# Attention ahead of two expert layers: value sums moved behind an earlier item's remainder on GpSimd, and half of the q loads moved to ScalarE's queue

## The chip, the cores and the metric

The program runs on one core of one Trainium2 chip. The metric is the device time of one execution in microseconds (us); lower is better. Engines are named as in the profile: PE is TensorE (PEld its weight loads), DVE is VectorE, ACT is ScalarE, POOL is GpSimd, SP is SyncE, which here only issues DMAs. Each engine runs its own instructions strictly in order, so an instruction that waits holds everything behind it on that engine.

## The reference, cut

Two attentions over q, k and v of shape (4, 8, 576, 64) are added: one over groups of four positions (averaged, then repeated four times), one over a band of seven neighbours. The sum goes through a layer of three projections with a maximum, and a layer of two projections with a product.

```python
out_up = np.repeat(sm_attn(q_d, k_d, v_d), 4, axis=2)   # q_d, k_d, v_d: means over 4 positions
mask = np.abs(pos[:, None] - pos[None, :]) < 4
scores = np.where(mask, scale * q @ k.T, -1e9)
out_local = softmax(scores) @ v
x = (out_up + out_local).transpose(0, 2, 1, 3).reshape(2304, 512)
h = np.maximum(np.maximum(x @ w1, x @ w2), x @ w3) @ w_out
out = ((h @ w_a) * (h @ w_b)) @ w_out2
```

## The kernel before

The attention is cut into 16 items, one for each batch and pair of heads. An item goes through five steps: `a_load_qk` and `a_load_v` issue its loads, `a_qk` makes transposed q and k and their sums over four, `a_scores` makes both score matrices and the softmax, `a_tr` transposes the probabilities and sums the values over four, `a_av` makes the weighted values, adds both attentions into `x32` and splits the sum into a rounded part `xh` (on ACT) and a remainder `xl` (on POOL). The main loop writes the steps of several items interleaved (`LOOP`, `LOOPS`); a list scheduler with its own timing model then sets the order on each engine. Pieces of the first expert layer's weights are loaded (`raw`), converted on DVE, ACT and POOL (`w_step`), and the first layer's matmuls for finished blocks of x (L700, through `early` and `fill`) stand between the attention's matmuls on PE. After the attention comes the rest of both layers, in an order written out by hand.

Items 8 to 15 load q and k already blocked for a transpose on DVE: four DMAs for k and four for q per item, of 72 KB each, in runs of 32 numbers (L228); items 0 to 7 are transposed on PE and take three DMAs for each (L236, L239). In the kernel before every load of the attention is issued from SP's queue. Buffers are few: the tiles q, k, vr and vw have one buffer in each of two pools, which even and odd items take in turn (`pool2`). Items 9, 11, 13 and 15 use a third pool, `ex2`, that no item before 9 uses. So a load of item i + 2 waits for the last reader of item i, and item 9 waits for nobody.

The values of an item stand in `vr` (for the sums over four) and `vw` (for the band). On POOL two additions sum vr: L419 adds the four rows in pairs, in place, and L420 adds the two halves into `vd`, which PE then reads (L456). The other work on POOL in this part: `ed` (L401) and `el` (L408) normalise the probabilities that PE then transposes (L430, L441), `xl` (L502) is the remainder, L567 the low part of a converted weight.

All loads count their completion on eight counters in turn, whichever queue issues them, and a load waits until the one eight places ahead of it in the program has landed. `tc.issue_after(x)` tells the scheduler to place what stands inside it behind instruction x.

Of the kernel before, what the change touches and what calls it, by code (L numbers as in the profile page):

```python
# [15 lines left out]
ALU = mybir.AluOpType  # L16
# [19 lines left out]

SPLIT_AFTER = {0: 1}
CB = 1

ACT_LOADS = 0  # L40
W2B = 4
# [23 lines left out]
def attn_moe_kernel(  # L65
# [14 lines left out]
    nc = tc.nc  # L80
# [35 lines left out]
    def nq(t):  # L116
        return min(QT, S - t * QT)
# [12 lines left out]
    def bk(st, name):  # L130
        if 1 in psp_:
            return psp_[1].tile([P, 512], F32, tag="m", name=name, bufs=4)
        t, n = ("t", 3) if st in "tv" else ("m", 5)
        return psp_[0].tile([P, 512], F32, tag=t, name=name, bufs=n)
# [25 lines left out]
    for half in range(2):  # L160
        m = cap[half * 64 : half * 64 + 64]
        for sgn in (1, -1):
            nc.gpsimd.affine_select(
                out=m,
# [26 lines left out]
    def xtiles(blk):  # L191
        if blk not in xh:
            pl = xps[blk // HB]
            xh[blk] = pl.tile([P, NK, TB], F32R, tag="xh", name="xh")
            xl[blk] = pl.tile([P, NK, TB], F32R, tag="xl", name="xl")
        return xh[blk], xl[blk]

    def pool(i, n):

        return ex if i < NI // 2 and i % n == n - 1 else ap_  # L200

    def pool2(i):

        return ex2 if i >= NI // 2 and i % 2 else pool(i, 2)

    def pieces(b):
        t0, done = b * S, 0
        while done < S:
            blk, o = divmod(t0 + done, TB)
            n = min(S - done, TB - o)  # L210
            yield done, n, blk, o
            done += n
# [4 lines left out]
    def a_load_qk(i):  # L217
        b, hp = items[i]
        s = st[i]
        h = 2 * hp  # L220
        engs = (nc.sync, nc.scalar if i < ACT_LOADS else nc.sync)
        if i >= TV:
            for nm, src in (("k", k), ("q", q)):
                x = pool2(i).tile([P, (RF + 1) * 2 * D], F32, tag=nm, bufs=1, name=nm)
                s[nm] = x[:, :S]
                for j in range(P // BS):
                    hh, d0 = divmod(j * BS, D)
                    nc.sync.dma_start(  # L228
                        x[j * BS : (j + 1) * BS, :S].rearrange("p (c d) -> p c d", d=BS),
                        src[b, h + hh, :, d0 : d0 + BS].rearrange("(c p) d -> p c d", p=BS),  # L230
                    )
            return
        for eng, nm, src in zip(engs, "kq", (k, q)):
            s[nm] = pool2(i).tile([P, RF + 1, 2, D], F32, tag=nm, bufs=1, name=nm)
            for j in range(2):
                eng.dma_start(  # L236
                    s[nm][:, :RF, j, :], src[b, h + j, : RF * P].rearrange("(r p) d -> p r d", p=P)
                )
            eng.dma_start(  # L239
                s[nm][:RT, RF], src[b, h : h + 2, RF * P :].rearrange("h p d -> p h d")  # L240
            )
# [45 lines left out]
    mark = {}  # L287
# [41 lines left out]
    def half_of(j, t):  # L329

        return 1 - j if t >= NP2 else j
# [83 lines left out]
    def a_tr(i):  # L415
        s = st[i]
        s["vd"] = ap_.tile([DK, NDK, 2, D], F32, tag="vd", bufs=2, name="vd")
        vr = s["vr"].rearrange("p h c f d -> p (h c) f d")
        nc.gpsimd.tensor_tensor(out=vr[:, :, 0:2, :], in0=vr[:, :, 0:2, :], in1=vr[:, :, 2:4, :], op=ALU.add)  # L419
        nc.gpsimd.tensor_tensor(  # L420
            out=s["vd"].rearrange("p c h d -> p h c d"),
            in0=s["vr"][:, :, :, 0, :],
            in1=s["vr"][:, :, :, 1, :],
            op=ALU.add,
        )
        ptd = s["ptd"] = pool2(i).tile([DK, NDK, NDQ * 2 * DQ], F32, tag="ptd", bufs=1, name="ptd")
        for c in range(NDK):
            ps = bk("t", "ps_td")
            for t in range(NDQ):
                nc.tensor.transpose(  # L430
                    ps[:DK, t * 2 * DQ : (t + 1) * 2 * DQ],
                    s["ed"][:, t, c * DK : (c + 1) * DK],
                    ident[: 2 * DQ, : 2 * DQ],
                )
            nc.scalar.copy(ptd[:, c, :], ps[:DK, : NDQ * 2 * DQ])
        pt = s["pt"] = []
        for u0 in range(0, NP2, TG):
            ps = bk("t", "ps_tl")
            n = min(TG, NP2 - u0)
            for u in range(n):  # L440
                nc.tensor.transpose(  # L441
                    ps[:, u * P : (u + 1) * P],
                    s["el"][:, 2 * (u0 + u) : 2 * (u0 + u) + 2, :].rearrange("m a x -> m (a x)"),
                    ident,
                )
            x = pool(i, 2).tile([P, TG, P], F32, tag="pt", bufs=3, name="pt")
            nc.scalar.copy(x[:, :n].rearrange("m t k -> m (t k)"), ps[:, : n * P])
            pt.append(x)

    def a_av(i):  # L450
        b, hp = items[i]
        s = st[i]
        ps = bk("v", "ps_ud")
        for c in range(NDK):
            for j in range(2):
                nc.tensor.matmul(  # L456
                    ps[64 * j : 64 * j + 64, :SD],
                    s["vd"][:, c, j, :],
                    s["ptd"][:, c, :].rearrange("m (t h i) -> m t h i", t=NDQ, h=2)[:, :, j],
                    start=(c == 0),  # L460
                    stop=(c == NDK - 1),
                )
        FH = FAC // 2
        up = pool(i, 2).tile([P, SD * 2, 1], F32, tag="up", bufs=1, name="up")
        nc.scalar.activation(
            out=up[:, :, 0].rearrange("m (g f) -> m g f", f=2),
            in_=ps[:, :SD].unsqueeze(2).to_broadcast([P, SD, 2]),
            func=AF.Copy,
            scale=1.0 / FAC,
        )  # L470
        x32 = pool(i, 2).tile([P, S], F32, tag="x32", bufs=1, name="x32")
        pss = [bk("v", "ps_av") for _ in AVG]
        for u in range(NP2):
            for j, r in ((0, 0), (1, 1), (1, 0), (0, 1)):
                t = r * NP2 + u
                half = half_of(j, t)
                rr = slice(r * KW, (r + 1) * KW)
                nc.tensor.matmul(  # L478
                    pss[r][64 * j : 64 * j + 64, u * QT : u * QT + nq(t)],
                    s["vw"][rr, j, u, :],  # L480
                    s["pt"][u // TG][rr, u % TG, half * 64 : half * 64 + nq(t)],
                    start=True,
                    stop=True,
                )
        for (g0, g1), ps in zip(AVG, pss):
            a0, a1 = g0 * QT, min(g1 * QT, S)
            if i in ADD_PSUM:
                mark['d', i] = nc.vector.tensor_tensor(
                    out=x32[:, a0:a1].rearrange("m (g f) -> m g f", f=FH),
                    in0=ps[:, : a1 - a0].rearrange("m (g f) -> m g f", f=FH),  # L490
                    in1=up[:, a0 // FH : a1 // FH].to_broadcast([P, (a1 - a0) // FH, FH]),
                    op=ALU.add,
                )
            else:
                nc.scalar.copy(x32[:, a0:a1], ps[:, : a1 - a0])
        if i not in ADD_PSUM:
            xg = x32.rearrange("m (g f) -> m g f", f=FH)
            mark['d', i] = nc.vector.tensor_tensor(out=xg, in0=xg, in1=up.to_broadcast([P, SD * 2, FH]), op=ALU.add)
        for o, n, blk, bo in pieces(b):
            a, l = xtiles(blk)  # L500
            nc.scalar.copy(a[:, hp, bo : bo + n], x32[:, o : o + n])  # L501
            nc.gpsimd.tensor_tensor(  # L502
                out=l[:, hp, bo : bo + n],
                in0=x32[:, o : o + n],
                in1=a[:, hp, bo : bo + n].bitcast(F32),
                op=ALU.subtract,
            )
        st[i] = None
# [18 lines left out]
    def convert_steps(key, w=None):  # L527
# [5 lines left out]
        pl = late["p"] if late_n[0] % 2 else rawp  # L533
        e = pl.tile([P, NP_], U16, tag="ce", name="ce", bufs=CB)
        fin = w
        if w is None or "c" not in psp_:
            m = pl.tile([P, NP_], F32, tag="cm", name="cm", bufs=CB)
            if w is None:
# [849 lines left out]
    def emit(f, i):  # L1388
        if i < NI and (f, i) not in emitted:
            emitted.add((f, i))  # L1390
            {"k": a_load_qk, "v": a_load_v, "Q": a_qk, "S": a_scores, "T": a_tr, "A": a_av}[f](i)
# [9 lines left out]
    for i in range(NI):  # L1401
# [4 lines left out]
        for x in LOOPS.get(i, LOOP).split():  # L1406
            f, d = x[0], int(x[1:])
# [121 lines left out]
    for n, (c, p) in enumerate(units):  # L1529
# [105 lines left out]
        if turn or p == 2:  # L1635
            x = 0 if turn else c + 1
# [38 lines left out]
```

## Time and profile before

| what | us |
|---|---|
| median of 3 runs | 848.06 (846.41 to 849.10) |
| the profiled execution, as timed | 848.16 |
| its span, first to last instruction | 846.4 |
| PE busy | 818.0 (97%) |
| DVE / POOL / ACT busy | 650.9 / 441.0 / 355.6 |

The timed value of the profiled execution is 1.8 us over its span and 0.1 us over the median. The attention ends near 200 us; from there on nearly all of the chain that ended last is PE. Where PE stands idle is in the first 110 us.

### The profile page before, as it was taken

The page shows a single profiled execution, that of the slowest core. Times are in us where ns is not written, and L with a number is a line of the kernel's source. Part 1 is how long each engine was busy: PE and PEld are TensorE (multiplying, and loading weights), DVE is VectorE, ACT ScalarE, POOL GpSimd, SP SyncE. Part 2 cuts the span into 40 slices and gives each one's busy share as a digit, 9 for nine tenths or more (in the row PEclk, how much of TensorE's full clock was granted, in tenths as well). Part 3 has the DMA queues.
Part 4 walks back from the last instruction along what each step waited for, and adds up shares of the span by engine and source line. Part 5 has one row for each costly group of instructions (what it writes and reads, how often), then busy time and mean ns, then how long its engine had stood idle before and what let it go on. Part 6 is the DMA issues. An engine that isn't in the chain of part 4 may idle for free.

```text
span 846.4 us, 15417 instructions
## 1 busy us (share of the span) xinstructions
PE 818.0 (97%) x5785; PEld 767.2 (91%) x5785; DVE 650.9 (77%) x1220; ACT 355.6 (42%) x812; POOL 441.0 (52%) x417
## 2 busy tenths in 40 slices
PE   5988799999999999999999999999999999999998
PEld 3767589999999999999989999999999999999997
DVE  4896986754989688689689689798888745577775
ACT  4785555544343223324246543444443432333331
POOL 3876586535456335546557645545554543355541
PEclk9699989999999999999999999999999999999999
DMA  7899975200321111320144554454442358766612
GB/s 175 182 191 163 171 124 110 43 21 2 124 75 50 51 50 50 137 75 26 68 156 174 189 189 168 179 187 171 178 174 106 143 207 330 259 225 224 225 51 74
DMA packets 125555, 116.33 MB, mean 137 GB/s; under 512 B 81834, under 2 KB 108202, under 8 KB 125482
## 3 DMA queue, kind: packets, MB, share of 16 engines
q1 hardware_dynamic: 121162, 98.06, 39.9%
q10 hardware_dynamic: 4320, 17.30, 5.7%
q8 instruction: 45, 0.74, 0.4%
q14 instruction: 28, 0.23, 0.1%
HBM read 80.74 MB, written 34.60 MB: 136 GB/s over the span
## 4 chain that ended last, share of the span: by engine, by line
PE 86%; DMA 5%; DVE 3%; POOL 3%; issue 1%; SPq 1%; ACT 1%; POOLq 0%; DVEq 0%; ACTq 0%
PE ps_m L700 40%; PE ps_u L1091 30%; PE ps_q L865 5%; PE ps_m L1241 4%; DMA vr<-in_v_dram 2%; PE ps_av L478 1%; PE ps_tl L441 1%; DMA raw<-in_moe_w_out_dram 1%; PE ps_ud L456 1%; PE ps_s L358 1%; PE ps_sd L340 1%; PE ps_m L865 1%; DMA vw<-in_v_dram 1%; POOL vr L419 1%; PE ps_td L430 1%
## 5 line engine op out<-in xcount | busy, mean ns | idle before, releaser
L700 PE MATMUL ps_m<-xh,w 128*128 128x384 f32 x864 | 173.7, 339 | 0.3 <-ACT xh L501 0.3
L700 PEld LDWEIGHTS ps_m<-xh,w 128*128 128x128 f32 x864 | 151.2, 189 | 1.7 <-ACT xh L501 0.6
L1091 PE MATMUL ps_u<-xh,w 128*128 128x384 f32 x720 | 136.8, 336 | 0.1
L1091 PEld LDWEIGHTS ps_u<-xh,w 128*128 128x128 f32 x720 | 125.3, 188 | 1.9 <-DVE acc L756 0.5
L1091 PE MATMUL ps_u<-xl,w 128*128 128x384 f32 x648 | 122.5, 335 | 0.4 <-ACT sn L1103 0.4
L1091 PEld LDWEIGHTS ps_u<-xl,w 128*128 128x128 f32 x648 | 112.9, 188 | 2.2 <-ACT sn L1103 0.7
L1103 ACT COPY sn<-ps_u 128x384 f32<-128x384 f32 x108 | 51.2, 479 | 123.5 <-PE ps_u L1091 120.3
L1281 POOL TENSOR_TENSOR gl<-g,gh 128x384 fp32r<-128x384 f32 x52 | 54.7, 1053 | 83.3 <-ACT gh L1280 83.3
L700 PE MATMUL ps_m<-xl,w 128*128 128x384 f32 x432 | 94.4, 337 | 0.2 <-POOL xl L502 0.2
L700 PE MATMUL ps_m<-wo,gh 128*128 128x512 f32 (+1 forms) x316 | 92.4, 390 | 0.0
L700 PEld LDWEIGHTS ps_m<-xl,w 128*128 128x128 f32 x432 | 76.5, 188 | 0.9 <-POOL xl L502 0.4
L700 PEld LDWEIGHTS ps_m<-wo,gh 128*128 128x128 f32 x316 | 58.4, 188 | 9.6
L729 DVE TENSOR_TENSOR t<-ps_m,t 128x384 f32<-128x384 f32 x48 | 26.4, 551 | 45.1 <-PE ps_m L700 38.4
L1022 POOL TENSOR_TENSOR w<-F,w 128x768 fp32r<-128x768 f32 (+1 forms) x36 | 56.3, 1578 | 9.2 <-ACT w L1020 8.7
L551 ACT ACTIVATE ce<-ce,ebias 128x512 int16<-128x512 uint16 x60 | 43.4, 723 | 41.0 <-DVE ce L544 41.0
L1350 DVE TENSOR_TENSOR acc<-ps_m,acc 128x512 f32<-128x512 f32 (+1 forms) x67 | 45.0, 677 | 18.7 <-PE ps_m L700 18.4
L554 DVE SCALAR_TENSOR_TENSOR ce<-raw,ce 128x512 uint16<-128x512 uint16 x60 | 49.8, 830 | 3.6 <-ACT ce L551 3.5
L1115 DVE TENSOR_TENSOR ca<-ps_u,sn 128x384 f32<-128x384 f32 x54 | 30.0, 555 | 28.8 <-PE ps_u L1091 17.9
L1033 POOL TENSOR_TENSOR F<-F 128x256 f32<-128x256 f32 x24 | 20.1, 839 | 59.3 <-DVE F L561 49.5
L700 PE MATMUL ps_m<-wo,gl 128*128 128x512 f32 (+1 forms) x158 | 48.9, 391 | 0.0
L1233 DVE TENSOR_TENSOR acc<-ps_m,acc 128x512 f32<-128x512 f32 (+1 forms) x62 | 33.3, 552 | 15.4 <-PE ps_m L1241 13.1
L544 DVE TENSOR_SCALAR ce<-raw 128x512 uint16<-128x512 uint16 x60 | 39.1, 652 | 2.1 <-DMA raw<-in_moe_w_dram 1.7
(209 smaller groups left out, 1684.6 us busy)
## 6 DMA issues: line engine op xcount, KB each, us to landing
dw<-w SPq DMA_DIRECT2D x24, 768.0 KB
raw<-in_moe_w_dram SPq DMA_DIRECT2D x18, 512.0 KB
raw<-in_moe_w_out_dram SPq DMA_DIRECT2D x18, 512.0 KB
w<-dw SPq DMA_DIRECT2D x12, 768.0 KB
w<-dw ACTq DMA_DIRECT2D x12, 768.0 KB
dw<-wo SPq DMA_DIRECT2D x12, 512.0 KB
vw<-in_v_dram SPq DMA_DIRECT2D x62, 80.0 KB
vr<-in_v_dram SPq DMA_DIRECT2D x16, 288.0 KB
```

Of the source, the lines that this page charges most:

```text
L544: nc.vector.tensor_scalar(out=e, in0=top, scalar1=0x7FF0, scalar2=None, op0=ALU.bitwise_and)
L551: nc.scalar.activation(out=s16, in_=e, func=AF.Relu, bias=ebias, scale=8.0)
L554: nc.vector.scalar_tensor_tensor(out=e, in0=top, scalar=0x8000, in1=e, op0=ALU.bitwise_and, op1=ALU.bitwise_or)
L700: nc.tensor.matmul(ps, lhs[a], rhs[b], start=(i == 0), stop=(i == n - 1))
L865: nc.tensor.matmul(ps, sw[c0, n][a][:, m * P : (m + 1) * P], hq[n][b], start=start and k == 0, stop=k == 2, skip_group_check=not start,)
L1022: nc.gpsimd.tensor_tensor(out=l, in0=w, in1=h.bitcast(F32), op=ALU.subtract)
L1091: nc.tensor.matmul(ps, w[:, a, slot, kk], y[:, b * HK + kk], start=start and i == 0, stop=i == 3 * HK - 1, skip_group_check=not start,)
L1103: nc.scalar.copy(t, ps)
L1233: nc.vector.tensor_tensor(out=a, in0=x, in1=a, op=ALU.add)
L1241: nc.tensor.matmul(y, lhs[a], tw[c, n][b], start=start and k == 0 and t == ts.start, stop=k == 2, skip_group_check=True,)
L1281: nc.gpsimd.tensor_tensor(out=l, in0=g, in1=h.bitcast(F32), op=ALU.subtract)
L1350: nc.vector.tensor_tensor(out=a, in0=ps, in1=a, op=ALU.add)
```

## The change

First, from item 6 on (`VR_AFTER`) both value additions of item i are placed behind the last remainder `xl` of item i - 2. Second, the four q loads of each of the items 8 to 15 are issued from ACT's queue; the k loads stay on SP's. No instruction is added or removed but the queue of 32 DMAs is another, and the scheduler orders all engines anew up to the end of the attention.

```diff
+VR_AFTER = 6
@@ a_load_qk, items 8 to 15
-                    nc.sync.dma_start(
+                    (nc.scalar if nm == "q" else nc.sync).dma_start(
@@ a_tr
-        nc.gpsimd.tensor_tensor(out=vr[:, :, 0:2, :], in0=vr[:, :, 0:2, :], in1=vr[:, :, 2:4, :], op=ALU.add)
-        nc.gpsimd.tensor_tensor(
...
+        after = ExitStack()
+        if i >= VR_AFTER:
+            after.enter_context(tc.issue_after(mark["x", i - 2].ins))
+        with after:
+            nc.gpsimd.tensor_tensor(out=vr[:, :, 0:2, :], in0=vr[:, :, 0:2, :], in1=vr[:, :, 2:4, :], op=ALU.add)
+            nc.gpsimd.tensor_tensor(
...
@@ a_av
-            nc.gpsimd.tensor_tensor(
+            mark["x", i] = nc.gpsimd.tensor_tensor(
                 out=l[:, hp, bo : bo + n],
```

POOL, from the normalisation of item 6 on (vr_1105 is item 6, vr_1304 item 7, vr_1638 item 9; x32_905, x32_1074 and x32_1220 are the sums of items 3, 4 and 5; line numbers of the changed kernel are six higher here). Before:

```order
L401 TENSOR_TENSOR ed_1015<-ed_1015,sd_1018 96x432
L419 TENSOR_TENSOR vr_1105<-vr_1105 72x4x128
L408 TENSOR_TENSOR el_1016<-el_1016,sl_1020 128x5x64 x2
L502 TENSOR_TENSOR xl_429<-x32_905,xh_428 128x384
L502 TENSOR_TENSOR xl_433<-x32_905,xh_432 128x192
L419 TENSOR_TENSOR vr_1304<-vr_1304 72x4x128
L419 TENSOR_TENSOR vr_1638<-vr_1638 72x4x128
L420 TENSOR_TENSOR vd_1415<-vr_1105 72x2x2x64
L567 TENSOR_TENSOR w6_781<-cm_1125,w6_780 128x512
L401 TENSOR_TENSOR ed_1277<-ed_1277,sd_1280 96x432
L502 TENSOR_TENSOR xl_433<-x32_1074,xh_432 128x192
L502 TENSOR_TENSOR xl_1102<-x32_1074,xh_1101 128x384
```

Now:

```order
L410 TENSOR_TENSOR el_1016<-el_1016,sl_1020 128x5x64 x2
L508 TENSOR_TENSOR xl_429<-x32_905,xh_428 128x384
L508 TENSOR_TENSOR xl_433<-x32_905,xh_432 128x192
L403 TENSOR_TENSOR ed_1277<-ed_1277,sd_1280 96x432
L410 TENSOR_TENSOR el_1278<-el_1278,sl_1282 128x5x64 x2
L403 TENSOR_TENSOR ed_1388<-ed_1388,sd_1391 96x432
L573 TENSOR_TENSOR w6_781<-cm_1125,w6_780 128x512
L508 TENSOR_TENSOR xl_433<-x32_1074,xh_432 128x192
L508 TENSOR_TENSOR xl_1102<-x32_1074,xh_1101 128x384
L425 TENSOR_TENSOR vr_1105<-vr_1105 72x4x128
L410 TENSOR_TENSOR el_1389<-el_1389,sl_1393 128x5x64 x2
L426 TENSOR_TENSOR vd_1415<-vr_1105 72x2x2x64
```

The additions of item 6 moved from ahead of item 3's remainder to behind item 4's; those of items 7 and 9 stood ahead of a weight piece, an `ed` and item 4's remainder and are no longer there.

SP at the very start, with the counters that each load waits for. Before:

```order
L236 DMA q<-in_q_dram 128x4x64 x2
L239 DMA q<-in_q_dram 64x2x64
L236 DMA k<-in_k_dram 128x4x64 x2
L239 DMA k<-in_k_dram 64x2x64 [waits DMAHW0_49]
L236 DMA q<-in_q_dram 128x4x64 [waits DMAHW1_49]
```

Now:

```order
L238 DMA q<-in_q_dram 128x4x64
L238 DMA q<-in_q_dram 128x4x64 [waits DMAHW0_49]
L241 DMA q<-in_q_dram 64x2x64 [waits DMAHW1_49]
L238 DMA k<-in_k_dram 128x4x64 [waits DMAHW2_49]
L238 DMA k<-in_k_dram 128x4x64 [waits DMAHW3_49]
L241 DMA k<-in_k_dram 64x2x64 [waits DMAHW4_49]
```

Item 9's four q loads now stand first on ACT's queue and take the counters 0, 3, 5 and 7, so the second q load of item 0 waits for the first of them.

ACT between the exponentials of item 6 and those of item 7. Before:

```order
L376 ACTIVATE ed,eps_119<-ps_sd,md 96x144 x3
L465 ACTIVATE up<-ps_ud 128x288
L566 CAST w_780<-cm 128x512
L395 ACTIVATE el<-el 128x5x64
L435 COPY ptd<-ps_td 72x288
L395 ACTIVATE el<-el 128x5x64
L283 ACTIVATE qd_95<-qp 64x3x48 x2
```

Now:

```order
L378 ACTIVATE ed,eps_119<-ps_sd,md 96x144 x3
L397 ACTIVATE el<-el 128x5x64
L230 DMA q<-in_q_dram 32x18x32
L441 COPY ptd<-ps_td 72x288
L397 ACTIVATE el<-el 128x5x64
L230 DMA q<-in_q_dram 32x18x32
L507 CAST xh<-x_905 128x384
L507 CAST xh<-x_905 128x192
L230 DMA q<-in_q_dram 32x18x32
L441 COPY ptd<-ps_td 72x288
L557 ACTIVATE ce<-ce,ebias 128x512
```

The q loads of item 10 now stand between the copies and exponentials; the first of them waits for DVE to have read item 8's q, and each for the load eight places ahead of it.

## Rows read from the trace of the kernel before

**Rows 1.** The page's part 2: busy tenths in 40 slices of 21.2 us.

```profile
PE   5988799999999999999999999999999999999998
PEclk9699989999999999999999999999999999999999
```

**Rows 2.** Stretches of 10 us: busy time of each engine, granted clock, DMA share, GB/s.

```profile
0.00:10.00 10.00, 3.29 (x13) 2.43 (x14) 1.85 (x4) 3.31 (x7) 6.00 (x24) 1.00 0.55 127
...
60.00:70.00 10.00, 10.00 (x156) 8.03 (x159) 8.55 (x24) 7.83 (x25) 6.13 (x8) 1.00 1.04 164
70.00:80.00 10.00, 8.85 (x122) 7.08 (x114) 5.96 (x14) 6.37 (x20) 5.66 (x8) 1.00 0.91 160
80.00:90.00 10.00, 5.18 (x95) 3.95 (x95) 8.82 (x19) 1.90 (x5) 6.24 (x7) 0.95 0.94 161
90.00:100.00 10.00, 9.67 (x130) 7.83 (x127) 9.06 (x21) 6.38 (x20) 7.00 (x7) 0.88 0.93 166
100.00:110.00 10.00, 7.43 (x36) 6.07 (x36) 10.00 (x23) 5.79 (x19) 7.24 (x8) 0.80 1.13 190
110.00:120.00 10.00, 10.00 (x127) 8.37 (x126) 7.80 (x22) 6.84 (x22) 8.25 (x10) 0.86 0.56 117
```

**Rows 3.** Waits, POOL alone, 60 to 110 us: total, times, longest.

```profile
POOL vr L419 <- DMA vr<-in_v_dram: 12.2, 4, 4.0
```

**Rows 4.** Timeline of POOL: start, us, instruction [idle before, releaser].

```profile
68.16 1.28 POOL L419 TENSOR_TENSOR vr<-vr 72x512 f32<-72x512 f32 x1 [3.87 <-DMA vr<-in_v_dram]
...
76.04 1.27 POOL L419 TENSOR_TENSOR vr<-vr 72x512 f32<-72x512 f32 x1 [3.72 <-DMA vr<-in_v_dram]
77.93 1.28 POOL L419 TENSOR_TENSOR vr<-vr 72x512 f32<-72x512 f32 x1 [0.62 <-DMA vr<-in_v_dram]
...
79.87 1.27 POOL L567 TENSOR_TENSOR w<-cm,w 128x512 fp32r<-128x512 f32 x1
81.10 0.91 POOL L401 TENSOR_TENSOR ed<-ed,sd 96x432 f32<-96x432 f32 x1
...
102.76 1.86 POOL L419 TENSOR_TENSOR vr<-vr 72x512 f32<-72x512 f32 x1 [3.97 <-DMA vr<-in_v_dram]
104.58 1.40 POOL L408 TENSOR_TENSOR el<-el,sl 128x320 f32<-128x320 f32 x2
```

**Rows 5.** Timeline of DVE.

```profile
81.18 1.11 DVE L547 TENSOR_SCALAR cm<-raw 128x512 uint32<-128x512 uint32 x1 [3.56 <-POOL w L567]
```

**Rows 6.** Timeline of PE: where it stood idle.

```profile
4.38 1.09 PE L309 MATMUL ps_t<-ident,k 128*128 128x128 f32 x4 [4.38 <-DMA k<-in_k_dram]
6.13 1.09 PE L309 MATMUL ps_t<-ident,q 128*128 128x128 f32 x4 [0.67 <-DMA q<-in_q_dram]
...
82.06 0.44 PE L430 MATMUL ps_td<-ident,ed 96*72 96x96 f32 x3 [0.95 <-POOL ed L401]
...
88.81 0.30 PE L345 MATMUL ps_s<-cap,identb 128*128 128x320 bf16 x1 [3.50 <-DVE el L392]
...
106.04 1.33 PE L441 MATMUL ps_tl<-ident,el 128*128 128x128 f32 x5 [2.45 <-POOL el L408]
```

**Rows 7.** Timeline of SP's queue: start, us of issuing.

```profile
0.74 0.99 SPq L236 DMA_DIRECT2D k<-in_k_dram  x2
...
2.53 1.14 SPq L236 DMA_DIRECT2D q<-in_q_dram  x2
...
60.28 1.20 SPq L228 DMA_DIRECT2D q<-in_q_dram  x2
61.57 2.07 SPq L228 DMA_DIRECT2D k<-in_k_dram  x4
63.74 0.42 SPq L248 DMA_DIRECT2D vr<-in_v_dram  x1
64.26 3.07 SPq L272 DMA_DIRECT2D vw<-in_v_dram  x4
67.37 3.31 SPq L228 DMA_DIRECT2D q<-in_q_dram  x6
70.78 1.67 SPq L248 DMA_DIRECT2D vr<-in_v_dram  x2
...
85.84 2.35 SPq L228 DMA_DIRECT2D q<-in_q_dram  x4
```

More of the change, by code (lines that the diff above doesn't have):

```diff
@@ L418, in a_tr @@
         vr = s["vr"].rearrange("p h c f d -> p (h c) f d")
-        nc.gpsimd.tensor_tensor(out=vr[:, :, 0:2, :], in0=vr[:, :, 0:2, :], in1=vr[:, :, 2:4, :], op=ALU.add)
-        nc.gpsimd.tensor_tensor(
[L421 to L425, printed above, removed]
+        after = ExitStack()
[4 more added lines that the diff above has]
+            nc.gpsimd.tensor_tensor(
+                out=s["vd"].rearrange("p c h d -> p h c d"),
+                in0=s["vr"][:, :, :, 0, :],
+                in1=s["vr"][:, :, :, 1, :],
+                op=ALU.add,
+            )
         ptd = s["ptd"] = pool2(i).tile([DK, NDK, NDQ * 2 * DQ], F32, tag="ptd", bufs=1, name="ptd")
```

## The prediction

> **What bounds the kernel now.** I read the page's slices first, then ten-microsecond stretches, then who waited for whom on POOL, DVE and PE, and last the timelines of POOL and SP around PE's idle places. The slices [rows 1] show PE full nearly everywhere but in the first five, some 106 us; that is the attention's first half. After 110 us PE has no room (10.00 of 10 us busy in the last stretch of [rows 2]), so a load or a POOL wait that gets shorter there moves nothing. What can be won lies before. In the stretches from 60 to 110 us PE is busy 10.00 + 8.85 + 5.18 + 9.67 + 7.43 = 41.1 of 50 us, so it is idle 8.9 us, and the granted clock falls to means of 0.95, 0.88, 0.80 and 0.86 from 80 to 120 us: parts of these stretches ran at 1.2 instead of 2.4 GHz, after idle pieces of 3.50 and 2.45 us [rows 2, 6]. If PE could use the whole of it, that would be (0.05 + 0.12 + 0.20 + 0.14) x 10 = 5.1 us more.
>
> Where do the idle pieces come from? Three of them, 0.95, 3.50 and 2.45 us, sum to 6.90 us [rows 6]. The reader should follow each back. At 102.76 POOL starts a value addition after 3.97 us of waiting for its load; `el` stands behind it and starts at 104.58, and PE starts on it at 106.04 [rows 4, 6]. At 76.04 and 77.93 two value additions wait 3.72 and 0.62 us; behind them stand a weight piece (79.87) and an `ed` (81.10). PE waited for that `ed` until 82.06. DVE waited 3.56 us for that weight piece, until 81.18 [rows 4, 5, 6], and everything on DVE behind it came later, the `el` for which PE waited until 88.81 among it. So additions whose loads came late held, on an in-order engine, work that was ready: 12.2 us of waiting in four places [rows 3]. The second thing to see is SP's queue. From 60.28 to 72.45 us its rows follow each other with gaps near 0.1 us: it issues all the time, at some 0.5 us for each load [rows 7]. The loads of vr come late because they stand in that row.
>
> **The change part by part.**
>
> The value additions from item 6 on. The order of POOL shows that items 6, 7 and 9 no longer stand ahead of `el`, the weight piece, `ed` and the remainders of items 3 and 4. Their two instructions still cost the same on POOL; what goes is the wait in front. By that time the vr load, issued long before, should have landed. Value: the three idle pieces of PE, -6.90 us. At the lower end of the gain stands 0, when what PE then waits for is the next late thing (k, vw or q through the same SP queue). The upper end is 6.90 + 5.1 = 12.0 us, if PE also keeps its clock. Queued behind the additions on POOL are now `el` and `hl`, and vd waits for them; PE needs vd of item i only after xl of item i - 2 and a whole item in between, so I cost that at nothing. It has one more reader: the vr load of item i + 2 waits for vd of item i, and on SP everything behind that load waits too. If that cover is gone the price is one such load, from 63.74 to the addition at 68.16, so 4.4 us [rows 4, 7].
>
> The q loads off SP. Each q load costs SP 1.20 / 2 to 3.31 / 6, near 0.57 us [rows 7]; a stretch of 60 to 73 us holds eight, 4.5 us. I give this no gain of its own. It is what lets vr, vw and k land sooner, so that the 6.90 us are really won and not turned into waits for loads.
>
> Here a rule speaks against the change. The row first: the DMA engines are busy for shares of 0.91 to 1.13 in these stretches, at 160 to 190 GB/s [rows 2]. The Trainium skill, DMA: Bandwidth & Descriptors, section Issuing engines are not separate DMA queues, says that loads started from several engines run on the same 16 DMA engines, and that a second issuer saves only the sequencer's time, which is "usually small relative to the DMA itself". By that rule the loads would land no sooner; SP's rows without gaps speak for the opposite, that issuing is the bound here. What the rule would make of the time is the first rival.
>
> The q loads onto ACT. No row shows such a load on ACT in this part. Of the 32, some 17 (four each of items 8, 10, 11, 12 and one more) fall before 110 us. At 0.5 us, SP's price for one, they take 8.5 us of ACT, which is busy 7.83 + 6.37 + 1.90 + 6.38 + 5.79 = 28.3 of 50 us from 60 to 110 us [rows 2] and has 21.7 us to spare. Most fall into gaps; but ACT is in order, and one load of each item stands ahead of a copy (ptd or pt) that PE reads. Five items by 0.5 us give +2.5 us, which I take, because ACT's spare time is well over the 8.5 us; the bounds are 0 and 8.5 us. What is queued behind: the copies and exponentials shown for items 6 and 7, and PE and DVE wait for these.
>
> The start. Item 9's q loads need no buffer to come free, so the scheduler put them first of all, on ACT, and the second q load of item 0 now waits for the first of them through the counters. Before, k of item 0 was issued from 0.74 and PE had it at 4.38; q was issued at 2.53 and, its second load, near 2.53 + 1.14 / 2 = 3.1, and PE had it at 6.13 [rows 6, 7]. If ACT's first load lands like k, near 4.3, the second q load starts 1.2 us later, and all of SP's queue behind it too. Value +1.2 us, since PE and DVE wait for loads all through the start. The bounds are 0 and 3.5 us: 4 x 72 KB more at 127 GB/s [rows 2] take 2.3 us, if nothing of the DMA engines' idle share (0.55 busy) hides them.
>
> **The sum** against the profiled execution's own 848.16 us (0.1 us over the median): 848.16 - 6.90 + 2.5 + 1.2 = 844.96. I forecast **845.0 us**, faster by 3.1 us or 0.37%. A measurement of this kernel can tell about 0.3%, 2.5 us, from no change, so this is close to that line.
>
> **The rivals.**
>
> First: the transfers are the bound, and the gain is used up by waits for loads. For it speak the DMA shares, and that DVE, too, is busy 42.4 of these 50 us [rows 2]; against it SP's rows without gaps. Then the 6.90 us are not won, the start costs 1.2 us, and the stretch from 60 us loses the four q loads of item 9, now at the start: 4 x 72 KB at 160 GB/s, 1.8 us. 848.16 + 1.2 - 1.8 = 847.6: no change. This is also the time by the skill's rule.
>
> Second, on the other side: ACT's in-order queue takes over the part that POOL had. A q load on ACT waits for the landing of the load eight places ahead, most of which SP issues, and for DVE's reading of the q two items back. When ACT gets there before SP's load has landed, it stands still, and with it exponentials and copies. A landing under load took 4.4 us (63.74 to 68.16) [rows 4, 7]. It decides from the point where the three items 10 to 12 lose together more than the 6.90 us, or 2.3 us each, half a landing. Then the wait is only handed on: 848.16 + 2.5 + 1.2 = 851.9, slower. For it: the loads stand amid exponentials, and SP is the late queue now. Against it: ACT has 21.7 us to spare, and SP is relieved.
>
> Third: the new order at the start costs its upper 3.5 us and the gain is halved: 848.16 - 3.45 + 2.5 + 3.5 = 850.7. That the change does not do what it says is excluded by the order of instructions.
>
> **How the numbers follow.** Forecast 0.52 (of that 0.46 below the line and 0.06 within), first rival 0.24 (0.02 faster, 0.18 same, 0.04 slower), second 0.16 and third 0.08 (together 0.03 same, 0.21 slower). Faster 0.48, same 0.27, slower 0.25. The range goes down to 848.16 - 12.0 + 2.5 + 1.2 = 839.9 and up to the second rival, 851.9; the tails beyond (ACT's bound of 8.5 us on top of the start) I hold for under 2 in 10.
>
> **What would show it.** Right: in the changed profile POOL's waits for vr between 60 and 110 us go from 12.2 us to under 3; PE's idle time in that stretch falls below 4 us; the stretches from 110 us look as before, but some 3 to 4 us earlier. PE's first transposes of q start 1 us or so later than 6.13. ACT's own queue shows issues of some 0.5 us, each with little wait ahead. Wrong: POOL's waits vanish and PE's idle time stays, with q, k or vw as the releaser (first rival); ACT stands idle ahead of q loads and PE waits for ptd, pt or qd (second); or the first 60 us take 3 us or more longer (third).

## The result, and the profile after

The changed kernel takes **856.62 us** (856.05 to 857.85) against 847.93 us before: ratio 1.0103, 95% interval 1.0085 to 1.0121, so it is slower by 8.7 us. The forecast was 845.0 us, with a range up to 851.9.

Where the time went is read best in three stretches. First the kernel before, then the changed one; columns as in [rows 2].

```profile
0.00:60.00 60.00, 45.69 (x548) 34.67 (x549) 46.30 (x118) 37.28 (x116) 37.91 (x57) 0.83 0.86 183
60.00:110.00 50.00, 41.13 (x516) 32.97 (x517) 42.39 (x99) 28.27 (x87) 32.27 (x36) 0.93 0.99 168
110.00:160.00 50.00, 50.00 (x605) 45.03 (x607) 37.23 (x96) 26.88 (x72) 31.70 (x37) 0.97 0.51 98
```

```profile
0.00:60.00 60.00, 38.20 (x461) 29.62 (x461) 41.00 (x105) 32.14 (x101) 33.38 (x52) 0.86 0.91 177
60.00:110.00 50.00, 43.90 (x577) 34.40 (x578) 43.47 (x104) 31.28 (x96) 32.26 (x36) 0.88 0.98 158
110.00:160.00 50.00, 46.69 (x537) 41.51 (x536) 35.15 (x82) 24.32 (x66) 28.93 (x34) 0.91 0.67 102
```

PE, the first number behind the comma, loses 7.5 us of busy time in the first 60 us, wins 2.8 us from 60 to 110, where the gain was forecast, and loses 3.3 us from 110 to 160, where before it had no idle time at all. Together that is 8.0 us, nearly the whole difference. The mean granted clock, the third number from the end, is lower than before in the second and third stretch too (0.88 against 0.93, 0.91 against 0.97), and no run shows what that adds. The slices, which answer [rows 1], show the thinner start too:

```profile
PE   4679899999999999999999999999999999999998
PEclk9889779999999999999999999999999999999999
```

What was forecast for POOL came true. Its two largest waits between 60 and 110 us (total, times, longest), and two of its moved additions (they answer [rows 3, 4]):

```profile
POOL el L410 <- DVE sl L409: 6.9, 3, 2.9
POOL xl L508 <- ACT xh L507: 5.1, 4, 2.4
```

```profile
90.75 1.28 POOL L425 TENSOR_TENSOR vr<-vr 72x512 f32<-72x512 f32 x1
...
100.11 1.53 POOL L425 TENSOR_TENSOR vr<-vr 72x512 f32<-72x512 f32 x1
```

In that stretch no addition waits for its load any more; before it was 12.2 us. The start came as described, too. ACT, SP and PE (the latter answers [rows 6]):

```profile
0.73 2.19 ACTq L230 DMA_DIRECT2D q<-in_q_dram  x4
```

```profile
2.54 1.83 SPq L238 DMA_DIRECT2D q<-in_q_dram  x2
```

```profile
4.92 1.09 PE L311 MATMUL ps_t<-ident,k 128*128 128x128 f32 x4 [4.92 <-DMA k<-in_k_dram]
7.52 1.12 PE L311 MATMUL ps_t<-ident,q 128*128 128x128 f32 x4 [1.51 <-DMA q<-in_q_dram]
...
29.83 1.03 PE L311 MATMUL ps_t<-ident,k 128*128 128x128 f32 x4 [3.30 <-DMA k<-in_k_dram]
```

The first two q loads of item 0 take 1.83 us to issue instead of 1.14, for the second waits for the counter, and PE's first transposes of q start 1.39 us later than before. But item 0's remainder on POOL starts at 42.21 us instead of 34.23:

```profile
42.21 1.79 POOL L508 TENSOR_TENSOR xl<-x,xh 128x384 fp32r<-128x384 f32 x2
```

That is 8 us, not 1.4. That gap is what the experiments had to explain.

### The profile page after: what moved, and what is told of

The parts are those of the page before. It is cut to its first block, busy times and chain, and to the rows that moved or that the text cites. A ratio compares the mean times of both kernels' runs of the same rounds, so it can differ in the third digit from the quotient of the medians.

```text
span 855.1 us, 15412 instructions
## 1 busy us (share of the span) xinstructions
PE 819.1 (96%) x5785; PEld 768.8 (90%) x5785; DVE 652.9 (76%) x1220; ACT 354.6 (41%) x812; POOL 441.0 (52%) x417
## 4 chain that ended last, share of the span: by engine, by line
PE 83%; DMA 6%; DVE 5%; issue 2%; POOL 2%; ACT 1%; SPq 1%; ACTq 0%; DVEq 0%; POOLq 0%
PE ps_m L706 39%; PE ps_u L1097 30%; PE ps_q L871 4%; PE ps_m L1247 4%; DMA vr<-in_v_dram 1%; DMA raw<-in_moe_w_dram 1%; DMA k<-in_k_dram 1%; DMA raw<-in_moe_w_out_dram 1%; PE ps_s L360 1%; PE ps_sd L342 1%; PE ps_m L871 1%; PE ps_av L484 1%; DMA q<-in_q_dram 1%; DMA vw<-in_v_dram 1%; PE ps_td L436 1%
## 5 line engine op out<-in xcount | busy, mean ns | idle before, releaser
L550 DVE TENSOR_SCALAR ce<-raw 128x512 uint16<-128x512 uint16 x60 | 41.3, 688 | 5.2 <-DMA raw<-in_moe_w_out_dram 4.0
```

Of the source, the lines that this page charges most:

```text
L550: nc.vector.tensor_scalar(out=e, in0=top, scalar1=0x7FF0, scalar2=None, op0=ALU.bitwise_and)
```

## Experiments

Ratios are to the kernel before, measured beside each run on the same chip; its median there was 846.6 to 847.9 us, so 0.1% is 0.85 us.

| run | q loads on ACT | additions moved | ratio | 95% interval |
|---|---|---|---|---|
| changed kernel | 8 to 15 | yes | 1.0103 | 1.0085 to 1.0121 |
| e1_vr_only | none | yes | 0.9928 | 0.9913 to 0.9943 |
| e2_q_only | 8 to 15 | no | 1.0082 | 1.0064 to 1.0101 |
| e3_q9_on_sp | 8, 10 to 15 | yes | 0.9983 | 0.9974 to 0.9992 |
| e5_only_q9 | 9 | no | 1.0127 | 1.0097 to 1.0156 |
| e7_q9_old_order | 9 | no, old order | 0.9991 | 0.9976 to 1.0006 |
| e8_new_order_no_q9 | none | no, order of e5 | 1.0141 | 1.0121 to 1.0162 |
| e10_one_place | none | no, one place of it | 1.0028 | 1.0013 to 1.0043 |
| e14_first_42 | none | no, first 42 us of it | 1.0039 | 1.0024 to 1.0054 |
| e15_first_100 | none | no, first 100 us of it | 1.0105 | 1.0085 to 1.0124 |
| e4_q9_held | 8 to 15, 9 late | yes | 0.9993 | 0.9979 to 1.0007 |
| e9_vr_q12 | 12 to 15 | yes | 0.9953 | 0.9935 to 0.9971 |
| e11_order_q_on_sp | none | yes, order of e3 | 0.9935 | 0.9916 to 0.9953 |
| e12_adds_alone | none | yes, old order else | 0.9939 | 0.9923 to 0.9956 |
| e13_vr_from_4 | none | from item 4 | 0.9954 | 0.9935 to 0.9973 |
| e16_q_order_adds | 8 to 15 | yes, order of e2 else | 1.0124 | 1.0104 to 1.0143 |

### Which part costs

The changed kernel taken apart: the additions alone, the q loads alone, both but for item 9's q, and item 9's q alone.

```diff
@@ e1_vr_only
-                    (nc.scalar if nm == "q" else nc.sync).dma_start(
+                    nc.sync.dma_start(
@@ e2_q_only
-VR_AFTER = 6
+VR_AFTER = 99
@@ e3_q9_on_sp
+                    (nc.scalar if nm == "q" and i != 9 else nc.sync).dma_start(
@@ e5_only_q9 (and VR_AFTER = 99)
+                    (nc.scalar if nm == "q" and i == 9 else nc.sync).dma_start(
```

> Only the value additions are moved (from item 6 on behind the remainder of the item two back); all q loads stay on SP. Before 847.9 us, changed 856.6 us. Theory A (the loss is made in the first 42 us by item 9's q loads, which start the program on ACT; the additions are worth what the trace of the changed kernel wins back between items 4 and 6, 3 to 5 us): 843 to 846 us. Theory B (the loss comes from q loads standing on ACT's in-order queue after 60 us): also 843 to 846 us, so this run does not part A from B. Theory C (the moved additions lose, since the vr and vw loads behind them on SP come later): 850 to 854 us.

> Only the q loads of items 8 to 15 are moved to ACT; the value additions are placed as before. Theories A and B: 857 to 861 us, all of the loss and without the gain of the additions. Theory C (the additions lose): 848 to 851 us.

> Both parts, but item 9's four q loads stay on SP, so ACT's queue starts without a load; items 8 and 10 to 15 load q from ACT. Theory A: the first 42 us are as before (item 0's remainder starts near 34.2 us on POOL, not 42.2) and the time is 844 to 848 us. Theory B: the start is as before, but ACT still waits with q loads after 60 us and the time is 852 to 857 us.

> The kernel before with one thing changed: item 9's four q loads on ACT, where they come first of all; everything else stays on SP and the additions stay where they were. Theory A: item 0's remainder starts 6 to 8 us later than 34.2 and most of that reaches the end: 853 to 857 us. Theory B: the start costs 1 to 2 us and the time is 848 to 850 us.

Measured: 840.75, 853.34, 844.98 and 857.24 us against 846.66. The additions alone gain 0.7%, 6.1 us by the ratio (5.9 between the medians), more than theories A and B had for them. Item 9's four q loads alone, the smallest edit of all, cost 1.3%: theory A in the time, and item 0's remainder starts at 41.62 us, 7.4 later; with those four on SP again it starts at 34.95. That the loss is made in the first 42 us, as theory A has it, is not shown by this, and comes out otherwise below. The other q loads on ACT cost too, from 0.9928 to 0.9983, so theory B has a share as well. Theory C falls for the additions alone, but comes back below. The q loads alone met no theory: at 853.34 us they cost less than A or B had, and less than item 9's four by themselves. The parts don't simply add; each of these kernels has an order of its own.

### Is it the loads, or the order?

Item 9's loads change two things: what is transferred at the start, and the order that the scheduler makes for everything else. A pair of kernels parts them. Every instruction of the attention is chained, engine by engine, to a given list; the loads at issue are left out of it. (Line numbers in chained kernels are some 240 higher, as the list stands ahead of the code.)

```diff
+        for names in ORDER:
+            last = None
...
+                    if last is not None:
+                        tc.add_manual_dep(i, last.name, dep, reason="order")
+                    last = i
```

> The kernel before with item 9's four q loads first on ACT's queue, as in the run that moved only them, but every other instruction of the attention is chained to the order that it has in the kernel before, engine by engine. Before is 846.7 us and the run with these loads and the scheduler's own order 857.2 us. Theory O (the new order is what costs; the loads themselves delay the start by 1.3 us, which DVE's backlog has swallowed by 17 us): 846 to 850 us. Theory L (the loads cost, by the transfer volume and the shared counters): 853 to 858 us.

> The other half of the same pair: no load stands on ACT, item 9's q loads are at their usual place on SP, but every other instruction of the attention is chained to the order that the scheduler makes when item 9's q loads come first. Theory O (the order costs): 853 to 858 us, with item 0's remainder on POOL 6 to 8 us later than 34.2. Theory L (the loads cost): 845 to 849 us.

The loads with the old order: 0.9991, no cost that can be told. The new order without the loads: 1.0141, 12 us, a little more than expected. Theory O holds on both sides. PE in the kernel with the loads and the old order, and after it the kernel before:

```profile
7.53 1.12 PE L548 MATMUL ps_t<-ident,q 128*128 128x128 f32 x4 [1.44 <-DMA q<-in_q_dram]
...
16.50 0.69 PE L669 MATMUL ps_td<-ident,ed 96*72 96x96 f32 x6 [0.85 <-POOL ed L640]
```

```profile
16.50 0.69 PE L430 MATMUL ps_td<-ident,ed 96*72 96x96 f32 x6 [1.85 <-POOL ed L401]
```

The transposes of q start 1.4 us late, and at 16.50 us both stand at the same place, after a wait that was there anyway (1.85 us, now 0.85). But the delay does not end there. With the loads and the old order, item 0's probabilities come to PE at 28.80 us instead of 27.00, and its remainder at 35.85 instead of 34.23:

```profile
28.80 1.33 PE L680 MATMUL ps_tl<-ident,el 128*128 128x128 f32 x5 [1.94 <-POOL el L647]
```

```profile
35.85 1.72 POOL L741 TENSOR_TENSOR xl<-x,xh 128x384 fp32r<-128x384 f32 x2 [0.96 <-ACT xh L740]
```

In the trace it is won back behind 60 us, where SP has four loads less to issue: the vr load of 98.81 us goes out at 96.19, and item 4's remainder starts at 79.12 us instead of 81.97. The 0.9991 is a small loss and a small gain together. Now PE between 26 and 36 us, in the new order without the loads, and before:

```profile
27.91 1.09 PE L548 MATMUL ps_t<-ident,k 128*128 128x128 f32 x4 [3.14 <-DMA k<-in_k_dram]
28.79 1.27 PE L680 MATMUL ps_tl<-ident,el 128*128 128x128 f32 x5
30.00 1.23 PE L695 MATMUL ps_ud<-ptd,vd 72*64 72x144 f32 x8
31.16 1.12 PE L548 MATMUL ps_t<-ident,q 128*128 128x128 f32 x4
...
32.50 1.76 PE L579 MATMUL ps_sd<-kd,qd 128*96 128x144 f32 x6
...
35.30 1.35 PE L717 MATMUL ps_av<-pt,vw 64*64 64x58 f32 x38
```

```profile
27.00 1.33 PE L441 MATMUL ps_tl<-ident,el 128*128 128x128 f32 x5 [0.57 <-POOL el L408]
28.28 1.09 PE L309 MATMUL ps_t<-ident,k 128*128 128x128 f32 x4
29.29 1.23 PE L456 MATMUL ps_ud<-ptd,vd 72*64 72x144 f32 x8
30.45 1.59 PE L478 MATMUL ps_av<-pt,vw 64*64 64x58 f32 x40
31.98 1.11 PE L309 MATMUL ps_t<-ident,q 128*128 128x128 f32 x4
```

In the new order item 3's transposes of k stand ahead of item 0's probabilities (`ps_tl`), so PE waits 3.14 us for that k; before, it worked on `ps_tl` while k came. The chain that ended last, in the new order, has this load on it:

```profile
23.91 3.87 DMA k<-in_k_dram
```

Further down, item 3's q and item 2's scores stand ahead of item 0's weighted values (`ps_av`), which come some 5 us later. Item 0's remainder on POOL, new order and before:

```profile
41.09 1.73 POOL L741 TENSOR_TENSOR xl<-x,xh 128x384 fp32r<-128x384 f32 x2
```

```profile
34.23 1.73 POOL L502 TENSOR_TENSOR xl<-x,xh 128x384 fp32r<-128x384 f32 x2 [0.93 <-ACT xh L501]
```

Behind the remainder stand the first layer's matmuls for that block, with which PE fills its idle places later.

How far does this one place carry? Three more orders, all with all loads on SP: the old one with only this place changed, and the new one cut at 42 and at 100 us, with the old one behind.

> The kernel before, all engines chained to its own order, but for one place on PE that is written as it stands in the order made when item 9's q loads come first: item 3's transposes of k stand ahead of the transposes of item 0's probabilities, and item 3's transposes of q, item 2's coarse scores and its two mask matmuls stand ahead of item 0's weighted values. No load moves. Chained to the whole of that order the kernel took 859.9 us against 847.5. If this place is where the order costs: 852 to 857 us, item 0's remainder 3 to 6 us later than 34.2. If the loss is spread over many places: 847 to 850 us.

> All loads on SP, no load moved. The order that the scheduler makes when item 9's q loads come first is kept on all engines up to item 0's last remainder (near 41 us); behind that everything stands in the order of the kernel before. The whole new order took 859.9 us against 847.5. In the profile of that run PE is busy 41.9 us of the first 60, against 45.7 before, and 45.3 us from 110 to 160, against 50. If the first 42 us make all of the loss: 856 to 860 us. If they make only the part that stands in the first 60 us, 3.8 us: 849.5 to 852.5 us. If later places make it: 846 to 849 us.

> As the run before, but the new order is kept up to item 5's last remainder (near 100 us). If the part from 110 to 160 us comes from the order in that stretch: as the run that keeps it up to 42 us, within 2 us. If it comes from what the first 100 us leave behind (matmuls of the first layer already used up, loads late): 856 to 860 us.

0.28%, 0.39% and 1.05%, against 1.41% for the whole. The place gives 2.4 us, the first 42 us 3.3, those up to 100 us 8.9. With the one place item 0's remainder starts at 37.81 us, 3.6 later, as expected, but the time falls into the second case, and so does that of the order kept up to 42 us. So the loss is spread: some 3 us up to 42 us and 6 more up to 100. The last 3 us, behind 100, rest on two intervals that just touch (1.0124 and 1.0121). PE from 60 us on in the run cut at 100 us:

```profile
60.00:110.00 50.00, 39.41 (x498) 32.51 (x495) 40.93 (x87) 24.89 (x74) 29.42 (x33) 0.84 0.78 137
110.00:160.00 50.00, 49.53 (x585) 43.90 (x582) 39.91 (x96) 29.32 (x82) 31.61 (x36) 0.96 0.68 123
```

Behind 110 us PE loses almost nothing here (49.53 against 50.00 us before; the whole new order has 45.27), so PE's idle time there comes with the order in that stretch, as the first case of the last expectation has it. The time, 856.08 us, lies all the same at the edge of the second case, because the order between 42 and 100 us costs, which neither case had. Which places in that order cost was not taken apart further. Why the scheduler's model chose this order when four loads came earlier was not tried.

### What the q loads cost on ACT

The other q loads, with item 9's out of the way.

> PE, DVE, POOL and ACT chained to the order of the kernel with both parts and item 9's q on SP (844.98 us, against 840.75 with all q on SP), but with all q loads back on SP. Theory H (ACT stands still ahead of q loads that wait for SP's loads): without them on ACT the 4.2 us come back, 839 to 842 us. Theory O (again the new order is what costs): 843.5 to 846 us.

With the order of the kernel that has seven items' q on ACT, but the loads back on SP, the time goes from 0.9983 to 0.9935, nearly that of the additions alone. Here it is the loads and not the order, 4.1 us for 28 loads: theory H. ACT with the loads, then in the same order without:

```profile
55.88 0.23 ACT L318 COPY kt<-ps_t 128x64 f32<-128x64 f32 x1
59.54 0.39 ACTq L230 DMA_DIRECT2D q<-in_q_dram  x1
60.03 0.58 ACT L325 COPY qt<-ps_t 128x512 f32<-128x512 f32 x1 [3.91 <-DMA k<-in_k_dram]
61.85 0.32 ACTq L230 DMA_DIRECT2D q<-in_q_dram  x1
62.22 0.21 ACT L326 COPY qt<-ps_t 128x64 f32<-128x64 f32 x1 [1.60 <-DMA k<-in_k_dram]
...
64.11 0.32 ACTq L230 DMA_DIRECT2D q<-in_q_dram  x1
64.53 0.39 ACT L441 COPY ptd<-ps_td 72x288 f32<-72x288 f32 x1 [1.53 <-DMA q<-in_q_dram]
```

```profile
54.87 0.22 ACT L556 COPY kt<-ps_t 128x64 f32<-128x64 f32 x1
55.33 0.59 ACT L563 COPY qt<-ps_t 128x512 f32<-128x512 f32 x1 [0.24 <-DVE qp L560]
```

Between the copy of kt and that of qt stands one q load of item 8. It waits for a load of SP's, and ACT stands idle 3.91 us, then 1.60 and 1.53: 7.0 us for one item, with 1.0 us of issuing in it. DVE pays in the same stretch:

```profile
66.21 0.60 DVE L399 TENSOR_REDUCE eps<-ed 96x3 f32<-96x432 f32 x1 [5.58 <-ACT ed L388]
```

Two variants, item 9's q on ACT but queued behind ACT's scaling of item 6's q, and q from ACT for items 12 to 15 only:

```diff
@@ e4_q9_held
+Q9_AFTER = 6
...
+                    if i == 9 and nm == "q":
+                        after.enter_context(tc.issue_after(mark["q", Q9_AFTER].ins))
@@ e9_vr_q12
+                    (nc.scalar if nm == "q" and i >= 12 else nc.sync).dma_start(
```

> Both parts of the change, all q loads of items 8 to 15 on ACT, but item 9's four are queued behind ACT's scaling of item 6's q (qd), near 60 us, and so don't start the program. If the placing at the start is the whole difference: as with item 9's q on SP, 843 to 847 us, with idle pieces of ACT ahead of q loads near 56 to 64 us. If ACT pays for item 9's loads too: 847 to 850 us.

> The additions moved as in the change; q from ACT only for items 12 to 15, whose loads fall behind some 110 us, where PE has no idle time; the q loads of items 8 to 11 stay on SP. The additions alone gave 840.75 us, and with items 8 and 10 to 15 on ACT 844.98. Theory H (ACT, in order, stands still ahead of a q load that waits for the load eight places ahead, and this costs only where PE has slack to lose, before 110 us): 840 to 842 us. If each q load on ACT costs its issue time wherever it stands: half of the 4.2 us, 842.5 to 844 us.

Held back, item 9's loads leave 0.9993: both parts of the change without its start are 1% faster than the changed kernel, and within the error like the run with item 9's q on SP. So the same four loads on the same queue cost little when they don't come first (0.9993 against 0.9983, intervals overlapping). The q loads of items 12 to 15 missed theory H: 0.9953, some 842.7 us, is what half of the cost would give. So loads behind some 100 us are not free, by themselves or by the order that the scheduler makes for them; these two were not parted there.

### What the additions are worth, and where that went

> The kernel before, all engines chained to its own order, but on POOL the two value additions of each item from item 6 on stand right behind the last remainder of the item two back. PE, DVE, ACT and SP keep the order of the kernel before. If the placing itself is the gain that the additions showed when the scheduler was free to order all engines anew (840.75 against 846.66 us): 840.5 to 843.5 us. If the gain came from the new order of the other engines: 846 to 849 us.

> All loads on SP and the additions moved from item 4 on instead of item 6; the scheduler orders all engines anew. The waits of POOL for vr between 14 and 60 us (5.1 us in the kernel before) are of items before 6. If the placing also pays there: 838 to 840.5 us; if those waits hold nothing that PE needs, 840 to 842 us; if vd then comes late for PE, or the new order is a bad one, over 843 us.

> The kernel with the q loads alone moved (853.34 us, against 846.66 before: +0.8%) with all engines chained to its order, but on POOL the two value additions of each item from item 6 on stand right behind the last remainder of the item two back. In that kernel POOL waits 9.1 us for vr between 60 and 125 us. If the placing is worth in this order what it was in the order of the kernel before (0.6%): +0.1 to +0.3% against before, some 848 to 849 us. If in this order PE is held by other things (q, k, late items) and the placing frees nothing: +0.7 to +1.0%, 852 to 855 us; that would be the gain that the changed kernel (+1.0%) does not show.

In the old order with nothing else moved the placing gains 0.6%, 5.2 us. In the order that the q loads bring about it loses 0.4% (1.0082 to 1.0124, intervals apart), 3.6 us, worse than either case expected. PE from 60 to 110 us, with the additions alone in the old order:

```profile
60.00:110.00 50.00, 44.92 (x597) 36.85 (x597) 45.68 (x104) 31.34 (x96) 33.19 (x38) 0.93 0.76 135
```

It is 3.8 us busier there than before, and 4.2 us over the first 160 us (141.03 against 136.83). Of the idle pieces of [rows 6] the one of 3.50 us is 1.27 us here, and those of 0.95 and 2.45 us, which ended with POOL, are gone. A difference between the two orders stands on SP. Its largest wait for vd from 60 to 160 us (total, times, longest): the kernel before, the additions alone in its order, the q loads alone, and these with the additions:

```profile
SPq L248 <- POOL vd L420: 17.5, 4, 8.7
```

```profile
SPq L488 <- POOL vd L660: 18.9, 4, 8.2
```

```profile
SPq L250 <- POOL vd L426: 8.1, 3, 5.0
```

```profile
SPq L493 <- POOL vd L669: 30.6, 7, 14.5
```

A vr load waits until the additions two items back have been made. In the old order moving them adds 1.4 us to that wait; in the other it adds 22.5 us, and the loads behind on SP wait too. There the remainders of items 4, 5 and 6, which the additions now stand behind, start at 92.30, 99.79 and 109.03 us instead of 74.61, 85.55 and 100.69. That these waits are what costs the 3.6 us is not shown: no run removes them, 14.5 of the 30.6 us are one wait behind 142 us, and the kernel before has 17.5 us of them. (In the changed kernel itself the scheduler had this in its plan, and SP's wait for vd is 5.5 us; what of its order costs there was not taken apart further.) From item 4 on instead of 6 the gain is not larger (0.9954), the third case of its expectation; whether vd or the order takes the rest was not tried.

The best kernel is the change without its second part: 840.75 us, faster than the kernel before and the changed one.

## Why the prediction was wrong, point by point

- **What bounds.** Right in kind: PE's idle places set the time. Over 160 us PE's busy time falls by 8.0 us in the changed kernel, with 8.7 us more in the result. Wrong in that only those before 110 us count: a kernel can make new ones behind, and this one has 3.3 us there. PE's idle time from 60 to 110 us fell from 8.9 to 6.1 us, not below 4, and the first 60 us took the sign that was named for the third rival.
- **The value additions, -6.90 us.** Right in the mechanism, and near in size in an order that stays as it is: -5.2 us there, -6.1 with the scheduler free. POOL's waits for vr went from 12.2 us to none.
- **vd costed at nothing, 4.4 us if its cover goes.** In the old order the additions gain in spite of it (SP's wait grows by 1.4 us); in the order that the q loads make they lose 3.6 us, with 22.5 us more of the wait that the step named, for the vr load on SP. The step took the cover from a trace whose order the change did not keep. How much of the changed kernel's loss is of this kind stays open.
- **The q loads off SP: "It is what lets vr, vw and k land sooner".** Not needed. The additions gain all of it with every load on SP, and less with q on ACT. Some time was saved on SP: with item 9's four loads gone from it a vr load went out 2.6 us sooner, near the 2.3 us of four issues at 0.57. That agrees with what the Trainium skill, DMA: Bandwidth & Descriptors, section Issuing engines are not separate DMA queues, says of a second issuer: it saves the sequencer's time only. With seven items' q on ACT it bought nothing at the end, as 844.98 against 840.75 us shows.
- **ACT, +2.5 us (0 to 8.5).** Measured 4.7 us without item 9's (0.9928 to 0.9983), 4.1 of it by the loads in the same order (0.9935 to 0.9983), so within the bounds, but by luck: the term counted issues, and the trace shows ACT standing still ahead of loads that wait, 7.0 us in item 8 with 1.0 us of issuing in it. This was the second rival's mechanism. Its price was too high: over items 10 to 12, which it counted, the idle pieces of ACT with a q load in them are at most 6.8 us in the run with item 9's q on SP, under the 6.90 it asked for, and the kernel stays faster than before. The half of the loads behind some 100 us cost too, so an issue price is not excluded.
- **The start, +1.2 us (0 to 3.5).** This is the step that failed. The delay itself was right (1.39 us at PE), and in the old order nothing of it is left at the end. The term priced four loads and left the new order that they bring about at zero, without a reason. That order, with the additions unmoved, costs 12 us without the loads (1.0141), and the loads without it nothing (0.9991). In the changed kernel item 9's loads at the start are worth 10.2 us (from 0.9983 to 1.0103) where the term had 1.2; the steps from run to run, -6.1, +4.7 and +10.2, give its +8.8 us by construction. That these 10.2 us too are the order is an inference: its own order was not run without the loads, but PE shows the same place there, item 3's k at 29.83 us after 3.30 us of waiting. The third rival named a new order at the start and its sign, a longer first 60 us, with a price of 3.5 us and a chance of 0.08. The first 42 us of the new order do cost 3.3 us, but the agreement is luck, for the price was worked out from the transfers; and it left out what the order costs behind.
- **Could it be seen before?** PE's order in the changed program already showed item 3's k ahead of item 0's probabilities. The prediction read the order at POOL, SP and ACT, where the diff acts, and not on PE between 20 and 40 us, where nothing was edited. It would have shown a sign and not the size: that place gives 2.4 of the 12 us.

## What to carry to other kernels

With a list scheduler, an edit costs by itself and by the order that it makes; the second can be far the larger, at places far from the edit (here 12 us against nothing that can be told). Read the new order first on the engine that sets the end, from the start, and part the two by chaining the old order to the new operation and the other way round. A DMA moved to a computing engine's queue can cost the wait that it has to make there, well over its issue (3.91 us with 0.39 of issuing above), so look at what it waits for before moving it.

## What the hardware showed that was not expected

Issuing a 72 KB load in runs of 32 numbers takes 0.32 us on ACT when it is issued alone (61.85, 64.11 us above), and 2.19 / 4, near 0.55 us, in the four at the start. SP needs near 0.57 us in a row of them [rows 7], and took 0.31 us for a single k load of that size (at 137.39 us in the changed kernel). So here the price went with the row and not with the engine. Four such loads and a waiting queue at the very start cost no measurable time at the end in the old order (0.9991, four issues less on SP behind 60 us included), although the DMA engines are then busy for 0.92 of the first 10 us instead of 0.55 [rows 2]. That kernel, with the old order:

```profile
0.00:10.00 10.00, 2.61 (x10) 1.72 (x10) 1.64 (x4) 2.67 (x6) 5.99 (x24) 1.00 0.92 147
```
